# Routed expert blocks on one core: parts of half a sequence, slots in units of 128, one-unit blocks at both ends

## The chip, the cores and the metric

One core of one Trainium2 chip runs the whole program. The metric is device time in microseconds (us), median of several executions. The profile is one execution, and its span can differ from the median time by some us. I compare runs of the same set (one chip, one sitting), and say so where a comparison goes beyond it.

Engines as the profile names them: PE is TensorE's products, PEld its weight loads, DVE VectorE, ACT ScalarE, POOL GpSimd, SP SyncE; a q behind a name is that engine's sequencer, which issues transfers.

## The reference

A causal convolution of 7 taps (softmax of 7 weights for each of 8 heads of 24 channels) over 8 sequences of 3584 tokens of 192 channels. Then each token is given one of 8 experts: its own best expert, or the one before it in its sequence, by a gate. The expert is a layer of two products with 1024 hidden values, scaled by the softmax value of the expert taken.

```python
for b in range(B):
    prev_e = -1
    for s in range(S):
        fresh_e = int(np.argmax(logits[b, s]))
        e = fresh_e if (s == 0 or local_gate[b, s] < 0.5) else prev_e   # cut
        prev_e = e
        h = np.maximum(x[b, s] @ w1[e], 0.0)
        out[b, s] = p[e] * (h @ w2[e])
```

All is fp32: 28,672 tokens, 1.57 MB of weights for an expert.

## The kernel before

Side work (the convolution mostly on VectorE, the routing, the scatter of token rows into `slots` in memory, ordered by expert) is done one sequence at a time. The slots of an expert come in blocks of 256, and a block loads its rows, its expert's weights, and computes. The side work of coming sequences is dealt out between the halves of the blocks' products, a fixed number of steps at a time.

```python
NT = S // P                      # 28 columns of 128 tokens: a sequence
BT = 256                         # slots in a block
NB = (N + E * (BT - 1)) // BT    # 119 blocks, whatever the routing is
wp = tc.tile_pool(name="wp", bufs=3)   # weights   (ctx.enter_context cut)
xp = tc.tile_pool(name="xp", bufs=3)   # rows of a block
op = tc.tile_pool(name="op", bufs=2)   # outputs of a block
# ... cut ...
def load(i):                     # SyncE: rows of the block, then its weights
    xg = xp.tile([P, KT, DG], F32, name="xg")
    get = nc.sync.dma_start(out=xg..., in_=slots...[bass.ds(r, 1)])
    wb = wp.tile([P, WA + WB], F32, name="wb")
    nc.sync.dma_start(out=wb, in_=w12[bass.ds(e, 1)]...)
# output(): second product, times the gate in xg, then for each 128 rows
    sent = nc.gpsimd.indirect_dma_start(out=out, in_=o_sb[:, k, :], in_offset=None,
        out_offset=bass.IndirectOffsetOnAxis(ap=xg.bitcast(I32)[:, k, 1:2], axis=0), ...)
# ... cut ...
PACE, BURST = 3, 3
for i in range(NB):
    ensure(i + AHEAD)            # AHEAD = 2: load(i + 2), unless done
    wb, xg = ready.pop(i)
    hT = hidden(wb, xT)          # 8 full and 8 half-height products, ReLU
    if i + 1 < NB:
        xT = turn(ready[i + 1][1])
    step()                       # side work
    output(wb, xg, hT)
    step()
```

The scatter of a block's outputs takes its indices from the block's row buffer `xg`. So a row buffer comes free only when that scatter has landed, and of row buffers there are three. The second product needs four evictions of the first one (ReLU, into `hT`), two on ScalarE and two on VectorE.

## Time and profile before

| | before |
|---|---|
| median time, first set (4 runs) | 1704.12 us (1701.16 to 1705.8) |
| profiled span | 1698.9 us |
| first expert block starts | 172.0 us |
| 119 blocks of 256 | 172.0 to 1690.7 us, 11.17 each where undisturbed |
| tail after the last product | 8.2 us |

The prediction below shows the lines by which it reads this. One view more, TensorE's waits in the whole span (engine, what its next instruction was to write, who released it: us in total, times, longest):

```profile
PE bg L218 <- DVE y_sb L194: 122.7, 4, 51.7
PE yps L483 <- DVE hT L474: 22.3, 9, 6.7
PE xps L448 <- DMA xg<-slots: 15.6, 2, 14.2
```

The first is the start: routing waits for the convolution. The second is TensorE waiting in mid-block for an eviction on VectorE.

### The profile page before, as it was taken

How to read it: one execution, taken by the hardware profiler on the slowest of the kernel's cores; microseconds unless marked ns; L12 is line 12 of the kernel's file. 1: busy time of each engine (PE TensorE's matmuls, PEld its weight loads, DVE VectorE, ACT ScalarE, POOL GpSimd, SP SyncE). 2: the span in 40 equal slices, each digit the busy share in tenths (PEclk: the TensorE clock that was granted, in tenths of full speed). 3: DMA queues.
4: the chain of work that ended last, by engine and by line, in shares of the span. 5: the costliest groups of instructions: out<-in, count | busy, mean ns of one | idle time of the engine just before them, and what ended most of it. 6: DMA issues, size and time to landing. Idle time of an engine off the chain costs nothing.

```text
span 1698.9 us, 23730 instructions
## 1 busy us (share of the span) xinstructions
PE 1460.1 (86%) x8900; PEld 1283.2 (76%) x8900; DVE 757.2 (45%) x1377; ACT 300.6 (18%) x559; POOL 562.6 (33%) x993
## 2 busy tenths in 40 slices
PE   0123899998498999899899899996999999999998
PEld 0012778886387888788788788885888998889987
DVE  4994327658368358447636821421221222212221
ACT  2021112222121122122113112110111111111111
POOL 0026353213723622742542361374111111111111
PEclk9966999999698999999899999997999999999999
DMA  4015555463363674575463465473544554545551
GB/s 166 12 79 188 200 192 215 171 254 108 117 250 144 209 274 147 200 260 187 162 215 146 166 220 184 166 239 139 186 171 178 190 190 165 190 171 187 185 187 52
DMA packets 59058, 299.93 MB, mean 177 GB/s; under 512 B 12602, under 2 KB 16156, under 8 KB 42560
## 3 DMA queue, kind: packets, MB, share of 16 engines
q1 hardware_dynamic: 35424, 243.99, 40.1%
q0 software_dynamic: 22944, 52.71, 8.7%
q8 instruction: 71, 1.16, 0.3%
q10 hardware_dynamic: 576, 1.72, 0.3%
q14 instruction: 43, 0.35, 0.1%
HBM read 245.43 MB, written 55.36 MB: 177 GB/s over the span
## 4 chain that ended last, share of the span: by engine, by line
issue 28%; PE 25%; POOL 11%; DVE 6%; DMA 1%; ACT 1%; POOLq 0%; another core or an unknown queue 0%; ACTq 0%; DVEq 0%
PE yps L483 12%; PE hps L459 7%; POOL out_dram L495 6%; PE hps L468 4%; POOL slots L333 3%; DVE y_sb L194 3%; PE bg L218 1%; PE xps L448 1%; POOL slots L415 1%; PE bg L227 1%; POOL apart L108 1%; DMA slots<-y_sb,posi 1%; DVE hT L474 0%; POOLq L495 0%; ACT y_sb L192 0%
## 5 line engine op out<-in xcount | busy, mean ns | idle before, releaser
L483 PE MATMUL yps<-wb,hT 128*128 128x192 f32 x3808 | 663.5, 333 | 32.5 <-DVE hT L474 22.3
L483 PEld LDWEIGHTS yps<-wb,hT 128*128 128x128 f32 x3808 | 635.8, 195 | 40.0 <-DVE hT L474 25.2
L495 POOL DMA_INDIRECT out_dram<-o_sb,xg x238 | 246.1, 1034 | 903.4 <-ACT o_sb L492 865.5
L459 PE MATMUL hps<-xT,wb 128*128 128x256 f32 x1904 | 440.2, 384 | 11.0 <-issue 6.1
L194 DVE SCALAR_TENSOR_TENSOR y_sb<-x_sb,c,y_sb 128x672 f32<-128x672 f32 (+1 forms) x432 | 375.3, 873 | 73.8 <-ACT y_sb L192 62.3
L459 PEld LDWEIGHTS hps<-xT,wb 128*128 128x128 f32 x1904 | 360.3, 192 | 61.7 <-issue 14.4
L474 DVE TENSOR_SCALAR hT<-hps 128x512 f32<-128x512 f32 x238 | 162.6, 690 | 307.6 <-PE hps L468 265.7
L333 POOL DMA_INDIRECT slots<-y_sb,posi x224 | 231.9, 1035 | 115.2 <-issue 65.1
L490 DVE TENSOR_SCALAR o_sb<-yps,xg 128x192 f32<-128x192 f32 x119 | 49.7, 417 | 480.8 <-ACT o_sb L492 466.0
L468 PE MATMUL hps<-xT,wb 64*128 64x256 f32 x1904 | 244.3, 391 | 11.6 <-issue 11.5
L468 PEld LDWEIGHTS hps<-xT,wb 64*128 64x128 f32 x1904 | 177.1, 187 | 70.3 <-issue 54.6
L476 ACT ACTIVATE hT<-hps 128x512 f32<-128x512 f32 x238 | 141.6, 597 | 472.1 <-PE hps L468 334.1
L492 ACT ACTIVATE o_sb<-yps,xg 128x192 f32<-128x192 f32 x119 | 50.1, 421 | 682.1 <-PE yps L483 556.3
L218 PE MATMUL bg<-ident,y_sb 128*128 128x128 f32 x224 | 35.8, 307 | 128.4 <-DVE y_sb L194 122.7
L218 PEld LDWEIGHTS bg<-ident,y_sb 128*128 128x128 f32 x224 | 29.3, 158 | 131.8 <-DVE y_sb L194 71.7
L448 PEld LDWEIGHTS xps<-ident,xg 128*128 128x128 f32 x476 | 50.7, 142 | 55.5 <-issue 38.1
L448 PE MATMUL xps<-ident,xg 128*128 128x128 f32 x476 | 79.1, 289 | 15.6 <-DMA xg<-slots 15.6
L451 DVE COPY xT<-xps 128x512 f32<-128x512 f32 x119 | 81.2, 682 | 18.5 <-remote 15.7
L220 ACT COPY yT<-bg 128x512 f32<-128x512 f32 x96 | 47.3, 535 | 117.9 <-PE bg L218 115.7
L192 ACT ACTIVATE y_sb<-x_sb,c 128x672 f32<-128x672 f32 (+1 forms) x72 | 55.0, 792 | 32.4 <-DMA slots<-y_sb,posi 26.1
L198 POOL COPY yr<-y_sb 128x1792 f32<-128x1792 f32 x8 | 13.8, 1722 | 101.7 <-DVE y_sb L194 94.1
L108 POOL MEMSET apart<- 1x1 f32 x478 | 43.1, 90 | 0.1
(119 smaller groups left out, 268.4 us busy)
## 6 DMA issues: line engine op xcount, KB each, us to landing
wb<-in_w_dram SPq DMA_DIRECT2D x119, 1536.0 KB
xg<-slots SPq DMA_DIRECT2D x119, 258.0 KB
x_sb<-in_x_dram SPq DMA_DIRECT2D x7, 3264.0 KB
out_dram<-o_sb,xg POOLq DMA_INDIRECT x238
slots<-y_sb,posi POOLq DMA_INDIRECT x224
x_sb<-in_x_dram SPq DMA_DIRECT2D x1, 1920.0 KB
x_sb<-in_x_dram ACTq DMA_DIRECT2D x1, 1344.0 KB
slots<-pad ACTq DMA_DIRECT2D x1, 258.0 KB
```

The costliest lines, as they stand in the source:

```text
L108: nc.gpsimd.memset(apart, 0.0)
L194: nc.vector.scalar_tensor_tensor(y, x_sb[:, t0 + k:t0 + k + n, hc], c[:, h, k:k + 1], y, Alu.mult, Alu.add)
L218: nc.tensor.transpose(tps[:, j, q * P:(q + 1) * P], src, identity=ident)
L333: put = nc.gpsimd.indirect_dma_start(out=slots[:, :], in_=y_sb[:, t, :], in_offset=None, out_offset=bass.IndirectOffsetOnAxis(ap=posi[:, t ...
L448: nc.tensor.transpose(xps[:, d, k * P:(k + 1) * P], xg[:, k, Y0 + d * P:Y0 + (d + 1) * P], identity=ident)
L451: nc.vector.tensor_copy(xT, xps)
L459: nc.tensor.matmul(hps[s // 2][:, s % 2, :], lhsT=wb[:, s * P:(s + 1) * P], rhs=xT[:, 0, :], start=(s % 2 == 0), stop=False, skip_group_ch ...
L468: nc.tensor.matmul(hps[half * 2 + row][:, j, :], lhsT=wb[rows, f0:f0 + P], rhs=xT[rows, 1, :], start=False, stop=True, skip_group_check=True)
L474: nc.vector.tensor_scalar(hT[:, 2 * q:2 * q + 2, :], hps[q], 0.0, None, Alu.max)
L476: nc.scalar.activation(hT[:, 2 * q:2 * q + 2, :], hps[q], Act.Relu)
L483: nc.tensor.matmul(yps[:, k, :], lhsT=hT[:, m, k * P:(k + 1) * P], rhs=wb[:, WA + m * D:WA + (m + 1) * D], start=(m == 0), stop=(m == FK - 1))
L495: sent = nc.gpsimd.indirect_dma_start(out=out, in_=o_sb[:, k, :], in_offset=None, out_offset=bass.IndirectOffsetOnAxis(ap=xg.bitcast(I32)[ ...
```

## The change

The intent: let the first block start earlier, by routing half a sequence (1792 tokens) at a time and sharing the convolution of the first two parts with TensorE; waste fewer slots, by units of 128 in place of 256; use one-unit blocks where few tokens are sorted yet (35 first) and for the remainder (22 last), with 87 two-unit blocks between; and deal side work by its estimated VectorE time, finishing sooner.

```diff
-NT = S // P
+UT = 128
+NT = 14
+NPART = N // PT                       # 16 parts of 1792 tokens
-NB = (N + E * (BT - 1)) // BT
+NU = (N + E * (UT - 1)) // UT         # 231 units
+EARLY = 3
+ONE = [_sure(min(g + 1, EARLY) * PT, UT) for g in range(NPART)]
+TWO = [_sure((g + 1) * PT - ONE[-1] * UT, BT) if g >= EARLY else 0 for g in range(NPART)]
+REST = NU - ONE[-1] - 2 * TWO[-1]
...
-    xs = ctx.enter_context(tc.tile_pool(name="xs", bufs=2))
-    ys = ctx.enter_context(tc.tile_pool(name="ys", bufs=2))
+    xs = ctx.enter_context(tc.tile_pool(name="xs", bufs=3))
+    ys = ctx.enter_context(tc.tile_pool(name="ys", bufs=4))
...
+        for i, h in enumerate(on_pe):              # three heads; parts 0 and 1 only
+            for k in range(KC):
+                nc.tensor.matmul(acc, lhsT=dg[:, i, k, :], rhs=chans(h, k),
+                                 start=(k == 0), stop=(k == KC - 1))
+    conv0 = conv(0, x_in.pop(0), ON_PE)
...
+    blocks = [(0, 1, i, ...) for i in range(ONE[-1])]
+    blocks += [(1, 2, i, ...) for i in range(TWO[-1])]
+    blocks += [(2, 1, i, NPART - 1) for i in range(REST)]
...
-    PACE, BURST = 3, 3
+    def step(time, scatters):          # side work worth `time` us, then
+        ...                            # up to `scatters` scatters
+    start_conv(ON_PE)
-        step()
-        output(wb, xg, hT)
-        step()
+        step(1.7 * n, 2 * n)
+        output(n, wb, xg, hT)
+        step(1.7 * n, 2 * n)
```

Here n is the number of units of the block. The buffers of weights (3), rows (3) and outputs (2) stay as they were.

## The prediction

> **What bounds the kernel now**
>
> I read the page's totals and slices first, then the busy time by window, then the chain of waits, the groups by shape, and last the queue waits and a timeline of the stalls. The slices:
>
> ```profile
> PE 1460.1 (86%) x8900; PEld 1283.2 (76%) x8900; DVE 757.2 (45%) x1377; ACT 300.6 (18%) x559; POOL 562.6 (33%) x993
> PE   0123899998498999899899899996999999999998
> DVE  4994327658368358447636821421221222212221
> ```
>
> TensorE is almost idle for four slices of 42.5 us, full from about slice 28, and has notches between. The windows put numbers to it (us, then PE, PEld, DVE, ACT, POOL busy, granted clock, DMA share, GB/s):
>
> ```profile
> 0.00:170.00 170.00, 30.36 (x199) 19.68 (x199) 119.02 (x230) 30.05 (x58) 46.57 (x76) 0.82 0.30 112
> 400.00:470.00 70.00, 36.16 (x193) 31.64 (x190) 42.63 (x93) 11.43 (x20) 37.36 (x65) 0.73 0.34 121
> 1130.00:1690.00 560.00, 547.03 (x3282) 487.49 (x3281) 116.50 (x201) 77.48 (x144) 125.78 (x240) 0.98 0.49 174
> ```
>
> Three stages with different limits: 170 us before the first block of experts, ruled by VectorE (119 us busy); a mixed stage to 1130 with stalls; and a stage where only expert blocks run. There the chain of waits repeats every 11.17 us (start, us, what); its pieces elsewhere give the parts of a block:
>
> ```profile
> 1191.43 8.61 issue
> 1202.60 8.61 issue
> ...
> 880.31 3.46 PE hps L459 x16
> 883.76 1.93 PE hps L468 x16
> 887.15 5.20 PE yps L483 x32
> ```
>
> 3.46 + 1.93 + 5.20 is 10.59, and four transposes with their hand-over make 0.58: 11.17. TensorE streams through it, so a block of 256 slots costs 11.17 us and nothing else can shorten that stage. 119 blocks make 1329 us. The last product ends at 1690.7 of 1698.9, a tail of 8.2. What is left, 1699 - 170 - 1329 - 8 = 192, is routing on TensorE (336 transposes at 0.109, 384 narrow products at about 0.06 and small ones: 74 us in all, 9.2 per sequence, some 60 after 170) and about 130 us of stalls, some of it at half clock. The worst stall, TensorE and then the load queue:
>
> ```profile
> 435.30 1.97 PE L218 MATMUL bg<-ident,y_sb 128*128 128x128 f32 x8 [12.17 <-DVE y_sb L194]
> 463.81 1.11 PE L448 MATMUL xps<-ident,xg 128*128 128x128 f32 x4 [14.16 <-DMA xg<-slots]
> SPq L431 <- DMA slots<-y_sb,posi: 36.0, 1, 36.0
> ```
>
> This is block 21 (170 + 21 * 11.17 = 405), the first that needs the third sequence. The side work wasn't done: at 3 convolution steps per half block, 48 steps are 8 blocks and about 20 routing steps are 10 more, against 14 blocks that a sequence feeds. The other notches (535, 685, 820, 960) have GpSimd saturated by the scatters of 28 columns:
>
> ```profile
> 542.10 7.83 PE L483 MATMUL yps<-wb,hT 128*128 128x192 f32 x28 [6.74 <-DVE hT L474]
> 125.83 1.60 POOL L333 DMA_INDIRECT slots<-y_sb,posi  x1 [0.21 <-issue]
> 145.80 0.96 POOL L333 DMA_INDIRECT slots<-y_sb,posi  x1 [0.21 <-issue]
> ```
>
> [...]5.20 / 32 is 162 ns for 192 columns, and each fp32 product is two such instructions (3808 for 119 * 16 products). The measurement is what I use; 128 columns then cost 109 ns, as the eight transposes from 599.54 to the next group at 600.41 do, each with its own 128x128 weight load. [...]a convolution step takes 952 ns for 672 elements and 595 for 336, so 238 ns are fixed. [...]a scatter takes 1.60 us beside convolution steps and 0.96 without. [...]the trace moved 442 GB/s in the 10 us from 740[...].
>
> **The change part by part**
>
> Slots in units of 128. 231 units replace 119 * 2 = 238: 7 * 5.585 = 39 us less for TensorE. Off the path that sets the end: nothing, this is the path.
>
> Blocks of one unit first (35) and last (22), 87 of two between. Each block still loads 8 + 8 weights for the first layer, twice, but streams half the columns. A pass of 128 columns with a fresh load takes 109 ns (above), and the half-height pairs of L468 run side by side, so a single should take 16 * 0.109 + 8 * 0.115 + 16 * 0.162 + 2 * 0.109 = 5.5, say 5.7 with hand-overs, against 5.585: 57 * 0.1 = 6 us given back. Traffic: 144 instead of 119 expert loads of 1.57 MB.
>
> Parts of half a sequence. The first block needs the convolution and routing of 1792 tokens instead of 3584; but 16 routings of about 45 small VectorE operations instead of 8, and 5.3 us of TensorE work each. Convolution steps: 14 * 48 + 2 * 30 = 732 at 0.59 = 432 us of VectorE instead of 375, with room for it once blocks run.
>
> The start. The taps' weights are asked for first (now they land at 21.1 behind 6.5 MB of x) and 2 MB of x suffice: start at about 9 instead of 23. VectorE: 30 steps of 0.583 (38.46 / 66), to 27. TensorE: 42 passes of 336 columns for part 0, 0.282 each, the first cold, 10 to 24; then part 1's, which stand ahead of routing in its order, to 35. Transposes and logits to 42. The routing chain on VectorE, 8.3 us of small operations at 0.2 to 0.4 and seven interleaved steps, to 54; the table to 59; the rest of part 1's steps to 72. Routing of part 1 then puts its last TensorE instruction at about 89, and the first block's transposes stand behind it. Part 0's 14 scatters end near 78, its block is loaded by 87 (2.7 us for rows and 6.3 for weights after issue, from the first load of before). First block near 90 instead of 170: 80 us.
>
> Budget and order of side work. A part costs 36 of budget at some 3.5 per half block, 5.2 double blocks, and feeds 7; so it runs ahead and the stalls of the kind at 405 to 465 should go. Scatters of 14 columns instead of 28 halve the GpSimd bursts.
>
> New stalls, estimated. In singles VectorE has 8 steps of 0.583 and three evictions of 0.4, 5.9 us per block of 5.7, in about 35 blocks: 7 us. A burst of 14 scatters at 1.9 (1.60 and the gap) plus outputs is 30 us of GpSimd over 3.5 singles of 20, a backlog of 10 against a slack of about 1.5, since a buffer of rows comes free only after its output landed: 3 parts, 25 us. x loads of 2 MB in the same queue ahead of weights: 3 times 3 to 4, 10. Waits of TensorE on side results, 3; cold first block, 2.
>
> Sum: 90 + 1290 (231 * 5.585) + 6 + 14 * 5.3 = 74 + tail 7 (one eviction and one scatter instead of two) = 1467; plus 47 = 1514 in the profile. The timed median lies 6 above the profiled span now, so 1520.
>
> **The rivals**
>
> Singles bound by transfers: 1.57 + 0.13 + 0.10 MB in 5.7 us is 316 GB/s, and with scatters and x about 360 early. For it: one load is in flight at a time behind the wait for the output, and the kernel averages 177. Against: 400 to 442 were reached in bursts. If only 260 can be held, 7 us per single, 57 * 1.3 = 74 more: about 1590.
>
> Singles bound by weight loads: if half-height loads don't pair at 128 columns, L468 stays at 1.9, 57 * 0.95 = 54 more: 1570. Against: in the mixed and pure stages both loads of a pair start together.
>
> VectorE becomes the bound until the side work ends: filled to 10.6 of 11.17 us per double block, a late ReLU eviction holds TensorE, as at 542. If the budget undercounts by 15%, some 55 blocks lose 1 us: 1570. For: the budget says 0.5 for a step that takes 0.58. Against: routing on TensorE stretches these blocks to about 12.2.
>
> It goes better: no backlog, no lag, first block at 80: 1475.
>
> **Range and chances**
>
> 1520 is the middle. The fixed parts (1290 + 74 + 7) are counted from measured pitches and barely move; the start may be 10 either way, and the new stalls 10 to 100. So 1475 to 1570 should hold 8 in 10. Even two rivals together stay under 1670, so faster 0.97, within 2% 0.02, slower 0.01.
>
> **What would show it right or wrong**
>
> The first L459-like group at 85 to 95; in a single block 16 first-layer passes in about 1.75 us and the 16 half-height in about 0.95 (1.6 or more: weight loads bind); TensorE idle before transposes on row loads in the first 320 us (backlog), or on weights at over 400 GB/s (transfers); waits of second-layer products on VectorE's hT (budget); no wait of the load queue on scatters after the first two parts; 11.17 us per double block after the side work ends near 950; HBM read near 289 MB (25 more loads of 1.57, 5 of x). I am wrong if singles cost over 6.5, or if TensorE idles over 60 us after its first block.

## The result, and the profile after

The changed kernel took 1639.17 us (1632.67 to 1644.47, 4 runs) beside 1704.12 before, on a chip whose number is not recorded. Ratios in this document are the mean time of one kernel's runs over that of the other's in the same rounds, so not quite the ratio of the medians: here 0.9619, with a 95% interval of 0.9581 to 0.9657. The direction held, but the time lies 69 us above the top of the predicted range. The page's lines on the same things:

```profile
PE 1481.7 (90%) x9762; PEld 1309.5 (80%) x9762; DVE 844.4 (52%) x2118; ACT 335.7 (20%) x709; POOL 511.8 (31%) x553
PE   6369898879999989998998999899899999999887
HBM read 288.54 MB, written 53.49 MB: 209 GB/s over the span
```

TensorE is at work from the first slice and the four empty slices at the start are gone; the memory traffic is what was forecast (289 MB). But notches remain all through the middle, and the last three slices are below 9. The windows of the five stages (us, PE, PEld, DVE, ACT, POOL busy, granted clock, DMA share, GB/s):

```profile
0.00:97.00 97.00, 44.50 (x202) 29.43 (x203) 62.31 (x183) 18.48 (x42) 33.72 (x66) 0.77 0.47 174
97.00:376.00 279.00, 240.58 (x1922) 219.42 (x1922) 167.10 (x438) 66.50 (x160) 97.39 (x98) 0.95 0.74 265
376.00:1170.00 794.00, 756.96 (x4705) 663.04 (x4704) 516.89 (x1277) 180.41 (x359) 284.11 (x290) 0.98 0.56 200
1170.00:1482.00 312.00, 306.37 (x1844) 273.88 (x1843) 72.56 (x155) 43.80 (x82) 73.17 (x76) 0.99 0.52 186
1482.00:1633.00 151.00, 133.29 (x1097) 123.76 (x1095) 25.51 (x66) 26.33 (x67) 22.41 (x23) 0.99 0.67 238
```

TensorE idles 38 us in the early one-unit stage, 37 in the two-unit stage with side work, and 18 in the last stage where nothing but blocks runs. Busy time hides some loss too, since the ends of products are modelled. So I set the starts of the blocks' first products against the prediction, stage by stage. The prediction's terms, grouped by stage: 90; early 35 * 5.685 + 3 parts of routing at 5.3 + all 47 of new stalls = 262; two-unit 87 * 11.17 + 11 parts at 5.3 = 1030; last 22 * 5.685 = 125; tail 7. (The routing transposes stand 2 parts before the first block, 3 in the early stage, 11 in the two-unit stage.)

| stage | predicted | measured | difference |
|---|---|---|---|
| to the first block | 90 | 96.6 | +7 |
| 35 one-unit blocks | 262 | 279.6 | +18 |
| 87 two-unit blocks | 1030 | 1105.5 | +75 |
| 22 one-unit blocks | 125 | 151.0 | +26 |
| tail | 7 | 5.8 | -1 |
| span | 1514 | 1638.5 | +124 |

Against before, the start gave 75 us and the tail 2; from the first block to the last product it is 1536.1 us in place of 1518.7, so 17 were given back there although 7 units fewer are computed. TensorE's waits say where to look:

```profile
PE hps L585 <- DMA wb<-in_w_dram: 31.0, 22, 2.5
PE yps L610 <- DVE hT L601: 20.0, 10, 3.3
PE yps L610 <- ACT hT L603: 12.1, 5, 6.4
```

There are two different things here: weights that come late for one-unit blocks, and second products that wait for evictions.

**A one-unit block that runs freely** (TensorE's timeline: start, us, what):

```profile
118.84 1.95 PE L585 MATMUL hps<-xT,wb 128*128 128x128 f32 x16
120.72 1.16 PE L594 MATMUL hps<-xT,wb 64*128 64x128 f32 x16
121.81 0.44 PE L573 MATMUL xps<-ident,xg 128*128 128x128 f32 x2
122.09 2.77 PE L610 MATMUL yps<-wb,hT 128*128 128x192 f32 x16
124.69 1.95 PE L585 MATMUL hps<-xT,wb 128*128 128x128 f32 x16
```

From start to start it is 1.88 + 1.09 + 0.28 + 2.60 = 5.85 us, where 5.7 was predicted, so the half-height loads do pair. The block itself is not the loss.

**The evictions.** The chain of waits through one stall of the two-unit stage (start, us, what), and the evictions themselves with what ended their wait:

```profile
1028.23 1.62 PE hps L594 x8
1029.85 0.02 issue
1029.88 0.69 DVE hT L601
1030.57 4.28 another core or an unknown queue
1034.85 0.02 issue
1034.88 0.70 DVE hT L601
```

```profile
1032.73 0.60 ACT L603 ACTIVATE hT<-hps 128x512 f32<-128x512 f32 x1 [2.76 <-remote]
1034.88 0.69 DVE L601 TENSOR_SCALAR hT<-hps 128x512 f32<-128x512 f32 x1 [4.31 <-remote]
1035.62 5.20 PE L610 MATMUL yps<-wb,hT 128*128 128x192 f32 x20 [1.32 <-DVE hT L601]
```

TensorE's last half-height product of this block ended at 1030.16 by the profile's model. ScalarE, free since 1029.97, begins its second eviction at 1032.73 and VectorE, free since 1030.57, its own at 1034.88. Neither engine was busy: each waited for TensorE's completion, 2.6 and 4.7 us. The profile finds no product ending close to the release and calls it "remote"; the semaphore that both waited on is one that only TensorE raises in this trace. The ends of products are modelled in this profile, so whether the product or the word was late cannot be told from them.

Five of the stage's 14 late blocks are of this kind ("late" in this document: over 3 us longer than the undisturbed 11.17). In five others it is the eviction of the outputs on ScalarE that waits for the word, and VectorE then has its side work to do before the ReLU. Three lines of such a block, from 958.2 (ScalarE's eviction of outputs, seven convolution steps, the second product):

```profile
962.72 0.42 ACT L619 ACTIVATE o_sb<-yps,xg 128x192 f32<-128x192 f32 x1 [9.49 <-remote]
963.58 4.08 DVE L194 SCALAR_TENSOR_TENSOR y_sb<-x_sb,c,y_sb 128x336 f32<-128x336 f32 x7
968.31 6.30 PE L610 MATMUL yps<-wb,hT 128*128 128x192 f32 x28 [3.29 <-DVE hT L601]
```

In the last four TensorE itself is held up: some of its first-layer products start late with no releaser in the profile. In the whole two-unit stage that comes to 12.0 us:

```profile
PE hps L585 <- issue: 9.7, 14, 1.6
PE hps L594 <- issue: 2.3, 5, 1.1
```

And eleven of the late blocks contain one or two stretches of 3.4 us in which TensorE's granted clock was half; over the stage it averaged 0.98, which makes some 22 us (an estimate: 1105.5 us times the 0.02 that is missing). TensorE's idle time there is 42 us, so idle time and clock are most of the 75.

The kernel before has waits for late words too, fewer of them. VectorE's waits, first in the kernel before, then in the changed one:

```profile
DVE hT L474 <- remote: 11.4, 3, 4.6
```

```profile
DVE hT L601 <- remote: 39.6, 10, 6.5
```

### The profile page after: what moved, and what is told of

It reads as the page before. It is cut to its first block, busy times and chain, and to the rows that moved or that the text cites. A ratio compares the mean times of both kernels' runs of the same rounds, so it can differ in the third digit from the quotient of the medians.

```text
span 1638.5 us, 26104 instructions
## 1 busy us (share of the span) xinstructions
PE 1481.7 (90%) x9762; PEld 1309.5 (80%) x9762; DVE 844.4 (52%) x2118; ACT 335.7 (20%) x709; POOL 511.8 (31%) x553
## 3 DMA queue, kind: packets, MB, share of 16 engines
q8 instruction: 78, 1.28, 0.3%
## 4 chain that ended last, share of the span: by engine, by line
PE 47%; issue 32%; POOL 7%; DVE 5%; another core or an unknown queue 5%; DMA 4%; POOLq 0%; ACT 0%; SPq 0%; ACTq 0%; DVEq 0%
PE yps L610 19%; PE hps L585 14%; PE hps L594 7%; POOL out_dram L622 5%; DVE y_sb L194 2%; PE bg L269 2%; PE xps L573 2%; POOL slots L432 2%; PE hps L182 2%; DMA wb<-in_w_dram 1%; DMA out_dram<-o_sb,xg 1%; PE bg L280 1%; DMA x_sb<-in_x_dram 1%; DVE hT L601 1%
## 5 line engine op out<-in xcount | busy, mean ns | idle before, releaser
L610 PEld LDWEIGHTS yps<-wb,hT 128*128 128x128 f32 x3696 | 616.2, 195 | 54.9 <-DVE hT L601 23.7
L622 POOL DMA_INDIRECT out_dram<-o_sb,xg x231 | 233.9, 1012 | 904.5 <-ACT o_sb L619 825.6
L585 PE MATMUL hps<-xT,wb 128*128 128x256 f32 (+1 forms) x2304 | 441.9, 345 | 53.1 <-DMA wb<-in_w_dram 31.0
L585 PEld LDWEIGHTS hps<-xT,wb 128*128 128x128 f32 x2304 | 374.2, 195 | 100.1 <-issue 41.9
L194 DVE SCALAR_TENSOR_TENSOR y_sb<-x_sb,c,y_sb 128x336 f32<-128x336 f32 x732 | 420.3, 583 | 32.0 <-ACT y_sb L170 8.9
L601 DVE TENSOR_SCALAR hT<-hps 128x512 f32<-128x512 f32 (+1 forms) x288 | 165.5, 585 | 386.7 <-PE hps L594 328.7
L603 ACT ACTIVATE hT<-hps 128x512 f32<-128x512 f32 (+1 forms) x288 | 147.7, 513 | 521.2 <-PE hps L594 325.1
L594 PE MATMUL hps<-xT,wb 64*128 64x256 f32 (+1 forms) x2304 | 246.1, 351 | 4.0 <-issue 3.8
L576 DVE COPY xT<-xps 128x512 f32<-128x512 f32 (+1 forms) x144 | 83.2, 578 | 28.8 <-remote 20.1
L170 ACT ACTIVATE y_sb<-x_sb,c 128x336 f32<-128x336 f32 x122 | 68.9, 576 | 9.5 <-POOL y_sb L160 6.7
L273 ACT COPY yT<-bg 128x512 f32<-128x512 f32 x90 | 48.6, 588 | 37.0 <-issue 19.2
L269 PEld LDWEIGHTS bg<-ident,y_sb 128*128 128x128 f32 x256 | 30.5, 146 | 19.2 <-DVE y_sb L194 17.2
L182 PE MATMUL hps<-x_sb,wb 128*128 128x336 f32 x84 | 26.1, 476 | 14.7 <-DMA x_sb<-in_x_dram 14.7
L182 PEld LDWEIGHTS hps<-x_sb,wb 128*128 128x128 f32 x84 | 17.1, 205 | 23.2 <-POOL wb L154 14.9
```

Source lines behind the costliest of these rows:

```text
L182: nc.tensor.matmul(acc, lhsT=dg[:, i, k, :], rhs=chans(h, k), start=(k == 0), stop=(k == KC - 1))
L194: nc.vector.scalar_tensor_tensor(cols(h), chans(h, k), c[:, h, k:k + 1], cols(h), Alu.mult, Alu.add)
L269: nc.tensor.transpose(tps[:, j, q * P:(q + 1) * P], src, identity=ident)
L576: nc.vector.tensor_copy(xT[:, :, :n * P], xps[:, :, :n * P])
L585: nc.tensor.matmul(hps[s // 2][:, s % 2, w], lhsT=wb[:, s * P:(s + 1) * P], rhs=xT[:, 0, w], start=(s % 2 == 0), stop=False, skip_group_ch ...
L594: nc.tensor.matmul(hps[half * 2 + row][:, j, w], lhsT=wb[rows, f0:f0 + P], rhs=xT[rows, 1, w], start=False, stop=True, skip_group_check=True)
```

## The experiments

Four sets, each on one chip. The kernel before stood beside them in all: 1701.54 us on chip 15 (first set below), 1662.99 and 1663.54 on chip 4, 1664.12 on chip 12. The theories:

- **Load loop.** In one-unit stages a row buffer is held until the block's output scatter lands; that scatter lands late behind the weight load that is running; the next load waits for it. More row buffers cure it.
- **Scatter burst.** In the two-unit stage the loss comes with the scatters of a part, which the changed kernel lets out up to four per half block. Fewer at a time cure it.
- **Budget** (rival). VectorE has too much side work ahead of the evictions. Less per half block cures it.
- **Too many one-unit blocks** (rival). Their weight loads are the cost.

### Set on chip 15

The changed kernel itself did not run in this set. Where a run is set against it, its figures are those of the first result, whose kernel before took 1704 us against 1702 here.

**e1_spread**: half as many scatters at a time.

```diff
-        step(1.7 * n, 2 * n)
+        step(1.7 * n, n)          # both places
```

> Half as many scatters of rows per step: 4 instead of 8 in a block of two units, 2 instead of 4 in a block of one. Theory A (the stall of about 6 us in one block of each part is the burst of scatters, with which the outputs queue): the 10 stalls of the two-unit stage shrink from 60-80 us in total to under 25, so 0.965 to 0.98 of the changed kernel's 1639, about 1590. Theory V (the stall is VectorE's budget of side work being too long for the ReLU behind it): nothing changes in it, within 0.5% of 1639.

Measured: 1590.28 us, ratio 0.9361 (0.9325 to 0.9398), against the changed kernel's 0.9619. The two-unit stage fell from 12.71 to 12.22 us per block, and its blocks over 3 us late from 14 to 6; the last stage stayed at 6.85. So the pace of the scatters matters for the two-unit stage on this chip and not for the last one.

**e2_budget**: less side work at a time.

```diff
-        step(1.7 * n, 2 * n)
+        step(1.3 * n, 2 * n)      # both places
```

> The budget of VectorE per step cut from 1.7 to 1.3 per unit, scatters as they were. Theory V: the waits of second-layer products for VectorE's hT (20 us) mostly go and the two-unit stage loses its one stall per part, 30 us or more less, about 1600. Theory A: the stalls stay at about 6 us per part, the side work only lasts longer (until about 1400 instead of 1170); within 1% of 1639.

Measured: 1645.45 us, ratio 0.9682 (0.9646 to 0.9718); 12.80 per double block. Half of the budget theory came true: in the two-unit stage TensorE's waits for VectorE's hT fell from 19.2 to 9.1 us (those for ScalarE's rose from 2.6 to 9.5). But the stage did not get shorter, so side work ahead of the evictions passes a delay on and is not what makes it.

**e3_rows**: twice the buffers of rows and outputs.

```diff
-    xp = ctx.enter_context(tc.tile_pool(name="xp", bufs=3))
+    xp = ctx.enter_context(tc.tile_pool(name="xp", bufs=6))
-    op = ctx.enter_context(tc.tile_pool(name="op", bufs=2))
+    op = ctx.enter_context(tc.tile_pool(name="op", bufs=4))
```

> Six buffers of gathered rows instead of three, four of outputs instead of two; nothing else. Theory L (a block of one unit is slow because its load waits for a buffer of rows, which the output scatter of three blocks before frees, and that scatter lands only once the weight load in flight is through): the 22 last blocks go from 6.9 us each to about 5.9, 20 us less there, about 15 less in the 35 first, and the stalls where the output's buffer is waited for (every second part, about 5 us each) go: about 1580 to 1600. Theory B (loads of single blocks are bound by the rate of transfers): the last stage stays at 6.9 per block, total within 1% of 1639.

Measured: 1596.8 us, ratio 0.938 (0.9349 to 0.9411). The last stage fell from 6.86 to 5.87 per block, the free-running pitch, the early one from 7.99 to 7.34; the two-unit stage stayed at 12.73 with 15 late blocks (12.71 and 14 in the first result). Weights no longer appear among TensorE's waits, and the load queue waits for something else. The longest wait of the load queue, first in the changed kernel, then with more buffers:

```profile
SPq L551 <- DMA out_dram<-o_sb,xg: 968.7, 133, 27.4
```

```profile
SPq L565 <- PE yps L610: 678.3, 96, 18.1
```

Before, loads of rows waited for landed outputs; now loads of weights wait for the product that frees a weight buffer, which is what three weight buffers should give. (The kernel before has the first of these waits too, 1002.4 us in all, but there TensorE waited for weights only once, 3.9 us.) The pools of rows and outputs were doubled together; that rows were short is read from this wait. With that the load loop is shown. And since the two-unit stage did not move, its loss is another thing.

**e4_early1**: one part's share of one-unit blocks at the front (7) instead of three parts' (35).

```diff
-EARLY = 3
+EARLY = 1
```

> Only 7 blocks of one unit at the start instead of 35, 101 of two units instead of 87. Theory L or B (a single unit costs 8.0 us early, a unit in a two-unit block 6.4): 28 units less at the dear price, 30 to 45 us less, about 1600. Rival (the early single blocks are what keeps TensorE fed until enough parts are routed): TensorE waits for the rows of parts 2 and 3, and the total is the same or up to 40 us longer.

Measured: 1623.17 us, ratio 0.9538 (0.9503 to 0.9573), 16 us below the changed kernel and not the 30 to 45 expected. Its two-unit blocks cost 12.97 and 20 of 101 are late. The first two of these (24.5 and 23.2 us) contain TensorE's waits for routing steps on VectorE, as the rival said; nearly all of the others show the late words. The one-unit blocks are not the main cost.

### First set on chip 4

**e6_nope**: the first two parts' convolution on VectorE alone.

```diff
+    USE_PE = ()
-    conv0 = conv(0, x_in.pop(0), ON_PE)
+    conv0 = conv(0, x_in.pop(0), USE_PE)
-    start_conv(ON_PE)
+    start_conv(USE_PE)
```

> The first two parts convolved on VectorE alone, as all the others are; their 42 TensorE products, 84 instructions, are gone. If the split matters for the start: part 0 ends 18 steps of 0.583 later on VectorE (at 44 instead of 34), the routing waits for it instead of for TensorE (40.7), part 1 again 10.5 later; first block of experts 13 us later, near 110, total about 1652. Rival: TensorE's own 26 us of convolution, ahead of the routing in its order, cost as much as they save: first block at 97 within 4, total unchanged.

Measured: 1573.56 us, ratio 0.9459 (0.9441 to 0.9477). The first block starts at 112.4. The surprise was elsewhere: the two-unit stage took 11.88 per block with not one late block. This kernel has the changed kernel's bursts, so either its edit or this chip took the stalls away.

**e7_both**: e1 and e3 together.

> Half the scatters per step and six buffers of rows, four of outputs, together. If the two causes are separate, their gains add up: 49 from the first, 42 from the second, so about 1548; two-unit blocks 12.2 us each, last blocks 5.9. If both cure one thing, about 1585.

Measured: 1490.71 us, ratio 0.8957 (0.8942 to 0.8972): 6.43, 11.87 and 5.85 us per block in the three stages, and no late two-unit block. The two gains were measured on another chip, so this does not test whether they add up.

**e8_three**: as e7, with half as many scatters again.

```diff
-        step(1.7 * n, n)                  # before output
-        step(1.7 * n, n)                  # after it
+        step(1.7 * n, n)
+        step(1.7 * n, (n + 1) // 2)
```

> As before with even fewer scatters: 3 in a block of two units (4 in the other), 2 in a block of one. Theory A, dose: the 6 long two-unit blocks that were left shrink again, two-unit mean from 12.2 to about 12.0, total about 1535. Rival: what is left isn't the scatters, within 0.5% of the kernel with 4.

Measured: 1496.06 us, ratio 0.8989 (0.8974 to 0.9004), some 5 us behind e7: one late block of 17.1 us, in which TensorE waits 3.6 us for a routing step on VectorE. With no late blocks left in e7 on this chip, the dose that the run was for could not be tested.

**e10_burst**: twice as many scatters at a time as in the changed kernel.

```diff
-        step(1.7 * n, 2 * n)
+        step(1.7 * n, 4 * n)      # both places
```

> The suspected cost doubled: 16 scatters in a block of two units, 8 in a block of one, so that a part's 14 go out within one block. Theory A: the stalls get longer, more than 10 us per part instead of 6 to 8, total 1660 to 1690. Rival (a stall per part whatever the size of the burst): 1639 within 0.7%.

Measured: 1566.8 us, ratio 0.9421 (0.9405 to 0.9437), and one late block, 11.92 per double block. Here the burst theory met its own dose and failed: on this chip doubled bursts do not make the stalls. What lacked was the changed kernel itself on such a chip.

### Second set on chip 4

**r_after**: the changed kernel, unedited.

> The changed kernel as it is, a second time, so that it stands on one chip beside the three runs after it. The kernel before took 1704 and 1702 us in the first two sets of runs and 1663 in the third, which was on another chip, so the first thing to read is which kind of chip this is. Theory A (the two-unit stage loses some 80 us to TensorE completions that are recorded 2.5 to 5 us late while scatters run, and this belongs to the chip): on a chip where the kernel before takes about 1700, ratio 0.962, 12.7 us per double block, 14 or so double blocks that are over 3 us late; on one where it takes about 1663, ratio 0.942, 11.9 us per double block, at most 2 such blocks, and the last one-unit blocks still 6.8 us, since the load loop is the same on both. Theory B (the burst stalls belong to the kernel, and the third set differed because of its edits): 12.7 us and 12 or more late blocks on any chip.

Measured: 1558.99 us (1553.04 to 1560.17), ratio 0.9371 (0.9355 to 0.9387). The same kernel is 80 us faster than in the first result, while the kernel before is 41 us faster. Its stages: first block at 96.7; early 264.4; two-unit 1031.9, that is 11.86 per block and none late; last 152.6; tail 5.8. The group of second products in the page, first in the first result, then here (busy us, mean ns, then idle time before it and what ended most of that):

```profile
L610 PE MATMUL yps<-wb,hT 128*128 128x192 f32 x3696 | 653.9, 334 | 42.3 <-DVE hT L601 20.0
```

```profile
L610 PE MATMUL yps<-wb,hT 128*128 128x192 f32 x3696 | 627.1, 327 | 0.1
```

The 42 us of waits are gone with no edit at all, and the products' modelled busy time is 27 us less; in the two-unit stage no product starts late without a releaser and the granted clock averages 1.00. "Remote" releases of ScalarE and VectorE, as in the eviction lines of the first result, are in both kernels' traces of the first result, in every trace of chip 15 and in none of chips 4 and 12. So the 75 us of the two-unit stage belong to the chip (or to what else went on there), not to the kernel alone.

The load loop is here as it was. Timeline of the third to fifth of the last blocks (SPq L551 loads rows, L565 weights; POOL L622 sends outputs; PE L585 is a block's first product):

```profile
1405.01 0.33 SPq L551 DMA_DIRECT2D xg<-slots  x1
1405.53 0.97 POOL L622 DMA_INDIRECT out_dram<-o_sb,xg  x1 [4.88 <-ACT o_sb L619]
1405.57 0.33 SPq L565 DMA_DIRECT2D wb<-in_w_dram  x1
...
1412.72 0.33 SPq L551 DMA_DIRECT2D xg<-slots  x1
...
1413.29 0.33 SPq L565 DMA_DIRECT2D wb<-in_w_dram  x1
...
1420.21 1.02 PE L585 MATMUL hps<-xT,wb 128*128 128x128 f32 x7 [1.21 <-DMA wb<-in_w_dram]
```

The outputs were issued at 1405.53, at the same moment as weights of 1.57 MB. In the trace's packets the scatter's queue moves nothing from 1405 to 1410 while the weights' queue carries up to 442 KB in a microsecond; the outputs go from 1410 on, 4.7 us after their issue, and only at 1412.72 may the next rows be asked for, 7.2 us after the scatter was issued. The weights behind them follow at 1413.29, 7.7 us after the last ones and not the 5.85 that a block takes, and 6.9 us later TensorE is still waiting for them (1.21 us). Not every turn is so long: the last 22 blocks average 6.94 us. The packets of the first result show such a turn too: outputs issued at 1508.89, nothing on the scatter's queue before 1512.01, weights at up to 430 KB in a microsecond meanwhile, the next rows asked for at 1514.12. Why the outputs did not move earlier the traces do not show.

**r_both**: e7 again, beside it.

> Twice the row buffers and scatters dealt out evenly, again, beside the changed kernel. Theory A: the load loop is worth about 25 us at the end and 10 to 30 at the start on any chip; the spread halves the late completions on a 1700 chip and has nothing to do on a 1663 chip. So ratio to the kernel before 0.91 (some 1545 us) on the former with 12.2 us per double block, 0.896 (1491) on the latter with 11.9. Theory B: the same 0.896 on either.

Measured: 1490.48 us, ratio 0.8959 (0.8944 to 0.8974). Stage by stage against the changed kernel beside it: start 96.7 and 96.7, early 224.8 and 264.4, two-unit 1032.7 and 1031.9, last 128.8 and 152.6. On this chip both mends together are worth 68 us by the medians and 63 between the two profiled executions, all of it in the one-unit stages. Its chain of waits (shares of the span):

```profile
PE 66%; issue 24%; POOL 5%; DVE 4%; DMA 1%; POOLq 0%; ACT 0%; ACTq 0%; DVEq 0%
```

No transfer to speak of is left on it. In the first result's chain PE had 47%, and "another core or an unknown queue" 5%.

**r_burst**: doubled bursts, beside it.

> Scatters let out twice as fast as in the changed kernel, beside it on the same chip. Theory A: on a 1700 chip fewer, longer bursts, with each part's stall at least as long as before: within 15 us of the changed kernel, more likely above it; on a 1663 chip no difference over 5 us, and no late blocks. Theory B (the burst is the cause everywhere): 40 us or more slower than the changed kernel on any chip.

Measured: 1569.27 us, ratio 0.9433 (0.9409 to 0.9458): 10 us over the changed kernel, outside of what either theory had said but near the chip theory. The profiled executions differ by 15 us: 10 in the early stage (274.6 against 264.4) and 5 in the two-unit stage, which has one late block.

**r_nope**: e6 again, beside it.

> The first part's convolution on VectorE alone, beside the changed kernel. The prediction put 13 us on TensorE's share of that convolution (the first block 13 us later without it). If so the first block begins at 110 to 113 and the whole is 10 to 18 us longer than the changed kernel in the same rounds. Rival: the first tables wait on VectorE's and GpSimd's routing anyway and the whole differs by under 5 us.

Measured: 1573.71 us, ratio 0.9452 (0.9436 to 0.9468), 15 us over the changed kernel; the first block at 113.0 in place of 96.7. What TensorE waits for now:

```profile
PE bg L270 <- POOL yr L174: 49.0, 2, 27.2
```

TensorE's share of the first two parts' convolution is worth 15 us. The 13 us are those that I expected before e6; the prediction as recorded has no figure for this share, although the text above says so.

### Set on chip 12

**x_after**: the changed kernel once more, as the measure for the next three.

> The changed kernel, as the measure for the two kernels after it on whichever chip this is. On a chip where the kernel before takes about 1700: ratio 0.962 and some 14 late double blocks. On one where it takes about 1663: 0.937 and none.

Measured: 1554.33 us, ratio 0.9336 (0.9318 to 0.9354); 11.86 per double block, none late. A second chip without the stalls.

**x_twice**: from the fourth part on, each scatter issued twice, the second time into spare memory (13 parts of 14 scatters, not the 12 parts of the expectation).

```diff
+        if g >= EARLY:
+            more = nc.gpsimd.indirect_dma_start(
+                out=spare[:, :], in_=rows, in_offset=None,
+                out_offset=bass.IndirectOffsetOnAxis(ap=to, axis=0)).ins
+            ...
```

> From the fourth part on, each scatter is issued twice, the second time to spare memory that nobody reads (the result stays correct). GpSimd gets 12 times 14 more scatters of 1.28 us, 215 us in all, on an engine that is busy for a third of the time. Theory M (margin: the bursts' traffic makes completions late, and the quiet chip only has more room): on the quiet chip late blocks appear, 5 or more, and 20 us or more are added; on the 1700 chip the stalls grow by half or more (40 us and more). Theory C (the chip alone, not the amount of traffic): on the quiet chip under 10 us more and no late block but what the longer GpSimd queue explains (rows waiting for scatters of outputs); on the 1700 chip under 20 us more.

Measured: 1712.69 us, ratio 1.0289 (1.0269 to 1.0309): 158 us more than the changed kernel, slower even than before. Of that 144 are in the two-unit stage (13.52 per block, 18 late). It looks like a win for the theory of a margin; the waits of TensorE, then of the load queue, say otherwise:

```profile
PE xps L580 <- DMA xg<-slots: 119.4, 30, 11.6
PE hps L592 <- DMA wb<-in_w_dram: 47.3, 27, 3.6
```

```profile
SPq L558 <- DMA out_dram<-o_sb,xg: 1331.6, 154, 24.6
```

TensorE waits for rows, not for evictions, and no "remote" release occurs in this trace. The outputs stand behind 28 scatters in GpSimd's order instead of 14, so row buffers come free late and rows arrive late: the load loop again, now in the two-unit stage. The added scatters did not bring back what chip 15 shows.

**x_plain**: the same bytes added by a contiguous transfer from the same queue.

```diff
+        if g >= EARLY:
+            u = len(puts)
+            more = nc.gpsimd.dma_start(out=spare[u * UT:(u + 1) * UT, :], in_=rows).ins
+            ...
```

> As the run before, but the added transfer of each scatter is a contiguous one of the same 129 KB, with no indices. If the bytes written are what counts, it costs as much as the doubled scatters; if GpSimd's indirect scatters are, it costs under a third of them. If the doubled scatters cost nothing here, this must cost nothing too.

Measured: 1630.39 us, ratio 0.9794 (0.9758 to 0.9829): 76 us more than the changed kernel, half of what the scatters cost, which neither alternative had said. Again it is rows:

```profile
PE xps L579 <- DMA xg<-slots: 62.0, 22, 8.3
```

An added transfer held GpSimd 0.58 us and an added scatter 0.99. That fits a cost by GpSimd's time ahead of the outputs better than one by bytes, which were the same.

**x_early1**: both mends and EARLY = 1.

> Twice the row and output buffers, scatters dealt out evenly, and only one part's share of one-unit blocks at the front (7 in place of 35, so 130 blocks in place of 144 and 14 weight loads fewer). Double blocks cost 11.87 on the quiet chip where two single ones cost 12.84, so 14 us less: 1476 on the quiet chip if the second double block's tokens are ready in time. Rival: the first double blocks wait for the third part's routing, which gives the 14 us back: 1490 or more. On the 1700 chip some 15 us below the two mends alone, about 1535.

Measured: 1503.85 us, ratio 0.9033 (0.9015 to 0.905). Set beside 0.8959 of r_both (another chip, but the kernels before differ by 0.6 us) it gives back more than the 14 us it saves: 12.11 per double block, and 3 late blocks that hold 27 us. The rival expectation was right. The version to keep is e7_both, 1490 us and faster than both kernels.

## Why the prediction was right or wrong

**Right: what bounds it, and the start.** TensorE is the path; 231 units at 5.585 and the routing at 5.3 per part fit: on chip 4 the two-unit stage took 1031.9 us where 1030 follows from them. The first block came at 96.6 instead of 90, just outside the promised 85 to 95: TensorE's first convolution product started at 14.7 us, when x had landed, and not at 10, and VectorE's steps began at 15.3 and not at about 9. The 0.282 us for a pass of 336 columns and the slow beginning hold: the passes came 0.56 us apart from 15.4 to 18.8 and 0.28 apart from 19.5 on (at 0.83 ns per column between the 109 ns of 128 and the 162 of 192, 336 come to an estimated 0.281). The first block, for which 2 us were counted as cold, took 10.7 us to the start of the next, against 5.85 free-running; the granted clock in its 3 us from 97 was 0.50.

**Right but a little small: one-unit blocks.** Free-running they take 5.85 instead of 5.7. Sixteen first-layer passes take 1.88 us from start to start instead of 1.75, the half-height ones 1.09 instead of 0.95. The rival of weight loads that do not pair (1.6 or more) is out, and so is the rival of a bandwidth limit: with more row buffers the same blocks loaded the same bytes and ran at 5.85 to 5.87.

**Right in mechanism, in size partly by luck: the early backlog.** "a buffer of rows comes free only after its output landed" was named and sized 25 us, with 22 more for other stalls. The stage came to 264.4 us on chip 4 against 262. But the mends took 39.6 us out of it, so the loop cost more than 25 and the rest less than 22. The burst was also priced too high: 1.60 us for a scatter is that of one stretch where convolution steps run back to back, while the changed kernel's 224 scatters took 0.98 on average, 1.28 with the gap of 0.30, so 14 take some 18 us and not 27. In the first result the stage took 279.6 us; late words are there too (TensorE's longest wait for ScalarE's hT in it was 6.4 us).

**Wrong: the last 22 blocks at 5.7.** "a single should take ... say 5.7 with hand-overs" counted TensorE alone, and the row buffers' loop was applied to the early stage only, as if it needed a burst of scatters. It needs none: an output that moved nothing for 4.7 us beside the weight load in flight, then the next load's own time, came to 7.7 us against 5.85 in the timeline above, and to 6.86 and 6.94 on average over the 22 blocks of the two profiles. Measured 151.0 instead of 125, +26 on the first chip and +28 on chip 4; e3_rows brings it to 129.

**Wrong: no stalls in the two-unit stage, on the chip that decided.** The step is "Scatters of 14 columns instead of 28 halve the GpSimd bursts", which I let stand for the disappearance of the before-kernel's stalls; all 47 us of new stalls went to the early stage. The cause behind the stalls was read too narrowly. The one at 542 was VectorE running late, as quoted, but other evictions in the same trace had waited for TensorE's completion, and I took the whole stall budget for VectorE and GpSimd being late. In the trace of the first result evictions begin 4.7 us after the modelled end of the product that they wait for in the block shown, and 7.1 us in the worst (product's end 1176.38, eviction 1183.46). The two-unit stage came out 75 us longer there, and the late words are absent on chips 4 and 12, where the same kernel took 1559 and 1554 us, inside the range of 1475 to 1570. That the stalls depend on the chip could not be read from the one chip that I had; that there is a second kind of stall could.

**The VectorE rival** (1570) is out as the cause: e2_budget relieved VectorE and gained nothing. It is not out as a link: in five of the 14 late blocks VectorE's side work stands between the late word and the ReLU.

**Its own signs of being wrong** came in the first result: one-unit blocks over 6.5 us (7.99 early, 6.86 last), and TensorE idle for some 98 us after its first block where 60 was the limit. The side work also lasted longer than the 950 us forecast: the last table was made at 1192 us, and at 1104 on chip 4.

**What stays open.** Why TensorE's completions are recorded late, and some of its products start late, on chip 15 and the first chip. There they go with the scatters: at half the pace, on chip 15, 6 blocks were late where the first result had 14. On the other chips neither twice the pace nor twice the scatters produced any. What else ran on those chips is not in these traces, and e7_both has not run on such a chip.

## What to carry to other kernels

Ask of each buffer what its release waits for: here the last reader of a row buffer was a scatter on its way out, so the load loop was longer than a one-unit block (7.7 us against 5.85 in one turn), and with more buffers the last blocks ran at their own pace (5.87). Here shorter blocks tightened this loop in a stage with nothing else going on too: the last 22 took 6.86 us each. And before sizing a stall that ends on another engine, read what released that engine; if the profile finds no releaser on the core, run the unedited kernel on a second chip before explaining it.
